# Splitting float64 weights in an attention and MoE kernel: sign by a parametric relu, low bits on GpSimd, and a new order of the opening

## The chip, the cores and the metric

The kernel runs on one core of a Trainium2 chip. The metric is the device time of one execution in microseconds (us); lower is better. TensorE is written PE, its weight loads PEld, VectorE DVE, ScalarE ACT, GpSimd POOL and the queue of the DMAs SP.

## The reference

Attention with a window of 128 keys and a distance bias for 8 batches, 8 heads, 576 positions and head width 64, then a gated layer: up-projection (512 to 1024), relu, a convolution over 3 tokens, a sigmoid gate, down-projection (1024 to 512). q, k and v are float32; the three weights are float64 words that have to become float32 on the chip.

```python
scores = scale * np.matmul(q, k.transpose(0, 1, 3, 2))
mask = (rel >= 0) & (rel < window)
scores = np.where(mask, scores + bias[None], -1000000000.0)
attn = softmax(scores)                      # max taken off, 1e-9 in the sum
x = (attn @ v), heads side by side          # 8 x 576 tokens, 512 wide
h = np.maximum(x @ w_in, 0.0)
for k in range(K):
    conv_out += conv_w[k][None, None, :] * hp[:, k:k + S, :]
gate = 1.0 / (1.0 + np.exp(-conv_out))
return (h * gate @ w_out).astype(np.float32)
```

## The kernel before

The 4608 tokens are 36 tiles t of 128 tokens; 18 chunks of 256 tokens go through the gated layer in 4 steps s each, a step being 256 of the 1024 hidden columns. Nothing is scheduled by a planner: three tables of names (`OPENING`, `PERIOD`, `TAIL`) are walked from left to right by `emit`, each name issues its instructions, and every engine runs its own in that order, one after another. `OPENING` covers tiles 0 to 10 and steps 0 to 10 and has all the weight work in it; `PERIOD` is repeated for two tiles and four steps at a time and has none; `TAIL` ends the program. Names that the text below uses:

- `LH`, `LD`, `LV`: DMAs of q and k, and of v, of one tile (tiles rqk and rv). From tile 9 on `LD` is 16 small DMAs. There are 3 buffers for rqk and 4 for rv.
- `QU`, `QV`: transposes of q and k on PE, and their copy on ACT; `S`: scores on PE; `MP`, `MB`: mask and bias with the row minimum, on DVE; `X`: exponentials on ACT; `N`: scaling of a row by its reciprocal sum, on DVE, ACT (4 instructions) or POOL; `T`, `RL`, `SEL`: transposes on PE, copy on ACT, select on POOL; `AV`: attention times v on PE. For tiles 9 and up `TQ` (DVE), `HQ` (ACT) and `LQ` (POOL or DVE) take the place of the transposes.
- `UH`: up-projection of half a step on PE; `HH`, `Z`, `CA`, `CB`, `TH`, `GT`, `GH`, `GL`: relu, convolution, gate and its split on ACT, DVE and POOL; `D`: down-projection on PE. Steps 0 to 3 multiply with the float32 weights wg, and later steps with a high part (wi, wo) and a low part (wl).
- `I`: idle matmuls on PE.

A float64 weight block b is 128 rows of 512 pairs of 32-bit words (blocks 0 to 3 and 5 to 8 are w_in, 4 is the small convolution weight, 9 to 16 are w_out), and each goes through: `F` its DMA (tile wst, 6 buffers), `CL` a clamp of the high words on POOL (L177), `RS` a scaling of them by 2 to the minus 112 into wg on ACT or POOL (L190, L188), `SG` a product with zero on POOL that leaves only the sign (L194), or `SH` a shift on DVE (L198) for two blocks, `V` two instructions on DVE: the low word's top 3 bits or'd with the sign (L209 or L213, into PSUM for blocks 0 to 6, else in place), and wg shifted by 3 and or'd with that (L216). `H` (ACT) and `W` (DVE or POOL, L235) make the high and low part.

One line of the queue's behaviour matters: `F`, `LD`, `LV` and the stores all stand in one queue on SP, where a DMA that waits for its buffer holds up all that stand behind it.

Of the kernel before, what the change touches and what calls it, by code (L numbers as in the profile page):

```python
# [944 lines left out]
```

## Time and profile before

| | before |
|---|---|
| median of 3 runs | 571.19 us (568.5 to 572.06) |
| the profiled execution | 568.98 us |
| its span, first to last instruction | 567.3 us |
| busy: PE, DVE, ACT, POOL | 558.1, 463.2, 430.6, 394.8 us |
| instructions | 16990 |

The profile is of one execution. Its time is 2.2 us below the median of the three runs and 1.7 us above its own span. An engine's busy time is the time in which it had an instruction in hand.

### The profile page before, as it was taken

What the parts mean: (1) busy time and instruction counts of PE and PEld (TensorE: products, weight loads), DVE (VectorE), ACT (ScalarE), POOL (GpSimd) and SP (SyncE); (2) the same over time, 40 slices, a digit from 0 to 9 for tenths busy, and PEclk for the clock granted to TensorE, in tenths of its full rate; (3) what the DMA queues carried; (4) which work ended last, traced back from release to release, by engine and by line L of the source; (5) the groups of instructions that cost most, each with busy time, mean ns of one, the idle gap of its engine ahead of it and who ended that gap; (6) DMA issues with size and microseconds to landing.
All of it is one profiled execution on the core that took longest, in us unless ns stands there. A gap on an engine that the chain in (4) does not pass through costs nothing.

```text
span 567.3 us, 16990 instructions
## 1 busy us (share of the span) xinstructions
PE 558.1 (98%) x6121; PEld 490.0 (86%) x6121; DVE 463.2 (82%) x1474; ACT 430.6 (76%) x1225; POOL 394.8 (70%) x453
## 2 busy tenths in 40 slices
...
GB/s 196 260 251 138 258 36 76 99 70 160 134 156 139 131 164 125 175 121 173 124 177 124 172 125 174 125 175 125 174 123 171 125 171 79 150 112 25 16 11 66
DMA packets 141225, 76.63 MB, mean 135 GB/s; under 512 B 116412, under 2 KB 131028, under 8 KB 141140
## 3 DMA queue, kind: packets, MB, share of 16 engines
...
## 4 chain that ended last, share of the span: by engine, by line
PE 91%; DVE 4%; DMA 2%; issue 1%; SPq 1%; ACT 0%; DVEq 0%
PE o L801 34%; PE p L698 34%; PE sc L387 8%; PE av L592 7%; PE o L791 2%; DMA rqk<-in_k_dram 2%; PE sc L432 2%; DVE sc L458 1%; PE av L632 1%; PE p L693 1%; SPq L320 1%; DVE wg L216 1%; PE pt L330 1%; DVE e L476 1%; DVE low L209 0%
## 5 line engine op out<-in xcount | busy, mean ns | idle before, releaser
L698 PE MATMUL p<-ring,wi 128*128 128x256 f32 x1088 | 195.4, 281 | 0.0
L731 DVE SCALAR_TENSOR_TENSOR zp<-hh,cw,zp 128x256 f32<-128x256 f32 (+7 forms) x384 | 160.5, 418 | 41.5 <-ACT zp L716 34.0
L698 PEld LDWEIGHTS p<-ring,wi 128*128 128x128 f32 x1088 | 168.7, 188 | 3.3 <-issue 0.2
L698 PE MATMUL p<-ring,wl 128*128 128x256 f32 x544 | 152.3, 280 | 0.0
L767 POOL TENSOR_TENSOR gl<-z,gh 128x512 fp32r<-128x512 f32 x67 | 86.8, 1296 | 79.9 <-ACT gh L758 79.1
L484 ACT ACTIVATE e<-e,st 128x128 f32<-128x128 f32 x288 | 112.7, 394 | 17.7 <-DVE st L476 17.4
L801 PE MATMUL o<-wo,gh 128*128 128x512 f32 x270 | 110.3, 409 | 0.0
L801 PE MATMUL o<-wo,gl 128*128 128x512 f32 x270 | 105.7, 392 | 0.0
L801 PE MATMUL o<-wl,gh 128*128 128x512 f32 x270 | 105.6, 391 | 0.0
L698 PEld LDWEIGHTS p<-ring,wl 128*128 128x128 f32 x544 | 102.7, 189 | 0.0
L716 ACT ACTIVATE zp<-hh,cw 128x256 f32<-128x256 f32 x144 | 68.9, 478 | 30.8 <-DVE z L746 20.2
L508 POOL TENSOR_TENSOR e<-e,st 128x512 f32<-128x512 f32 x60 | 62.4, 1041 | 15.1 <-DVE st L496 14.9
L368 POOL TENSOR_TENSOR qkT_low<-blk,qkT 128x1024 fp32r<-128x1024 f32 x25 | 59.9, 2397 | 16.8 <-ACT qkT L361 10.5
L476 DVE CUSTOM_DVE_ANT_0 e<-sc,bias 128x128 f32<-128x128 f32 x288 | 69.0, 285 | 1.1 <-DVE sc L458 0.2
L738 ACT ACTIVATE zp<-zp 128x512 f32<-128x512 f32 (+1 forms) x73 | 42.1, 577 | 33.3 <-DVE zp L731 33.1
L801 PEld LDWEIGHTS o<-wo,gh 128*128 128x128 f32 x270 | 50.6, 187 | 13.8 <-issue 0.2
L746 DVE SCALAR_TENSOR_TENSOR z<-zp,hh 128x512 f32<-128x512 f32 (+1 forms) x73 | 49.3, 676 | 14.1 <-ACT zp L738 12.3
L801 PEld LDWEIGHTS o<-wo,gl 128*128 128x128 f32 x270 | 50.6, 187 | 11.6
L710 ACT ACTIVATE hh<-p 128x512 f32<-128x512 f32 x67 | 40.0, 597 | 26.2 <-PE p L698 24.1
L801 PEld LDWEIGHTS o<-wl,gh 128*128 128x128 f32 x270 | 50.8, 188 | 9.5
L458 DVE COPY_PREDICATED sc<-m_prev,sc 128x256 f32<-128x256 uint8 x128 | 50.9, 420 | 8.9 <-PE sc L387 6.4
L484 ACT ACTIVATION_READ_ACCUMULATOR e<-e,st 128x1 f32 x288 | 54.3, 188 | 0.0
...
## 6 DMA issues: line engine op xcount, KB each, us to landing
...
rr<-scr SPq DMA_DIRECT2D x112, 128.0 KB
...
rqk<-in_q_dram SPq DMA_DIRECT2D x216, 32.0 KB
rqk<-in_k_dram SPq DMA_DIRECT2D x216, 32.0 KB
...
```

The lines of the kernel that those rows point to most:

```text
L368: eng.tensor_tensor(out=turned_of(qkT_low, t), in0=blks[t], in1=hi, op=ALU.subtract)
L387: nc.tensor.matmul(to, turned_of(tq, t)[rows, 0, g, b], of, start=n == 0, stop=n == len(passes) - 1)
L458: nc.vector.copy_predicated(out=s_cur, mask=mask.unsqueeze(1).to_broadcast(shp), data=data)
L476: nc.vector.tensor_tensor_reduce(out=e[:, j, :], in0=s_cur[:, g, :], in1=bias[:, head_of(t, u * HU + j), :], scale=-0.125, scalar=FAR, op0 ...
L484: nc.scalar.activation(out=e[:, j, :], in_=e[:, j, :], func=AF.Exp, bias=st[:, 0, j : j + 1], scale=-1.0, accum_out=st[:, 1, j : j + 1],)
L508: eng.tensor_tensor(out=e, in0=e, in1=st[:, 2, :].unsqueeze(2).to_broadcast([P, HU, P]), op=ALU.mult)
L698: nc.tensor.matmul(ps, a[:, part], ring[:, i, cc, cols], start=cc == 0 and n == 0, stop=cc == NCC - 1 and n == 2)
L716: nc.scalar.activation(out=zps[s][:, ff, :], in_=hhs[s][:, ff, 1 : 1 + CW], func=AF.Copy, scale=cw[:, 1, f : f + 1])
L731: nc.vector.scalar_tensor_tensor(out=z[:, ff, a:cut], in0=hh[:, ff, a + kk : cut + kk], scalar=cw[:, kk, f : f + 1], in1=z[:, ff, a:cut], ...
L746: nc.vector.scalar_tensor_tensor(out=zgs[s][:, ff], in0=zps[s][:, ff], scalar=1.0, in1=hhs[s][:, ff, 1 : 1 + CW], op0=ALU.add, op1=ALU.mult,)
L767: eng.tensor_tensor(out=gl, in0=zgs.pop(s), in1=as32(gh), op=ALU.subtract)
L801: nc.tensor.matmul(to, a[:, ff, ms], w[:, part], start=first and n == 0, stop=end and n == 2)
```

## The change

`RS` runs on ACT for all 17 blocks, as a parametric relu: a positive word is scaled by 2 to the minus 112 and a negative one by that times minus 2 to the 32, which puts one more bit in the exponent field, and that bit is the sign after the shift by 3. `SG` and `SH` are gone. A new `LW` on POOL multiplies the low word, as an unsigned integer, by 2 to the minus 29, bounds it by 7 and writes it back rounded to an integer. `V` is one instruction on DVE, and reads both its inputs from SBUF. No block's low bits go through PSUM any more.

The tables of who does what change too: six of the seven `N` that were on ACT leave it (one other comes), `N` on DVE grows from 5 to 10 in the opening, `W` on POOL goes from 10 blocks to 8, both `LQ` of tiles 9 and 10 are on POOL, and the low part of the gate of step 7 goes to DVE. `OPENING` is a new order of the same pieces; the number of `I` matmuls is the same.

```diff
-    LOW_PSUM = {0, 1, 2, 3, 4, 5, 6}
-    SIGNS = {0, 1, 2, 3, 5, 6, 7, 8, 9, 10, 11, 12, 13, 15, 16}
-    LOW_POOL = {2, 3, 7, 8, 9, 10, 11, 13, 14, 16}
-    RB_POOL = {0, 1, 3, 4, 5, 7, 9, 15}
-    N_ACT = {(1, 0), (2, 0), (3, 0), (4, 0), (4, 1), (5, 0), (5, 1)}
-    N_POOL = {(6, 0), (6, 1), (7, 0), (7, 1), (8, 0), (8, 1), (9, 0), (9, 1), (10, 0), (10, 1)}
-    GL_DVE = set()
+    LOW_POOL = {6, 8, 10, 11, 13, 14, 15, 16}
+    N_ACT = {(8, 0)}
+    N_POOL = {(1, 1), (4, 0), (5, 0), (5, 1), (7, 0), (7, 1), (8, 1), (9, 0), (9, 1), (10, 0), (10, 1)}
+    GL_DVE = {7}
-    LQ_DVE = {9, 10}
+    LQ_DVE = set()
...
-        if b in RB_POOL:
-            nc.gpsimd.tensor_scalar(out=g, in0=hf, scalar1=2.0**-112, scalar2=1.0, op0=ALU.mult, op1=ALU.mult)
-        else:
-            nc.scalar.activation(out=g, in_=hf, func=AF.Copy, scale=2.0**-112)
-
-    def w_sign(b):
-        hf = wst[b][..., 1].bitcast(F32)
-        nc.gpsimd.tensor_scalar(out=hf, in0=hf, scalar1=0.0, scalar2=0.0, op0=ALU.mult, op1=ALU.mult)
-
-    def w_shift(b):
+        nc.scalar.activation(out=g, in_=hf, func=AF.Prelu, scale=2.0**-112, alpha=-(2.0**32))
+
+    def w_low(b):
         lo = wst[b][..., 0]
-        nc.vector.tensor_scalar(out=lo, in0=lo, scalar1=29, scalar2=None, op0=ALU.logical_shift_right)
+        nc.gpsimd.tensor_scalar(out=lo, in0=lo, scalar1=2.0**-29, scalar2=7.0, op0=ALU.mult, op1=ALU.min)
 
     def w_bits(b):
         st, g = wst.pop(b), wgs[b]
...
         nc.vector.scalar_tensor_tensor(
-            out=g, in0=g, scalar=3, in1=low, op0=ALU.logical_shift_left, op1=ALU.bitwise_or
+            out=g, in0=g, scalar=3, in1=st[..., 0], op0=ALU.logical_shift_left, op1=ALU.bitwise_or
         )
...
-    LH0.0 QU0.0 LH0.1 LD1 F0 LD2 QU0.1 F4 QV0.0 LD3 CL0 CL4 S0.0 MP0.0.0 MB0.0.0 QV0.1 S0.1 F1 QU1.0 MP0.0.1 MB0.0.1
+    LH0.0 QU0.0 LH0.1 LD1 F0 LD2 QU0.1 F4 QV0.0 LD3 CL0 CL4 S0.0 MP0.0.0 MB0.0.0 QV0.1 S0.1 MP0.1.1 F1 QU1.0 MP0.0.1
```

What the new order means is best seen in the engines' own rows (in them a name's first number is the tile or block, and the last the buffer). The first place is SP's queue from the third w_in block to the block with number 2, before and then now:

```order
L170 DMA wst5_249<-in_moe_w_in_dram 128x1024
L320 DMA rqk4_263<-in_q_dram 64x8x64 x2
L320 DMA rqk4_263<-in_k_dram 64x8x64 x2
L320 DMA rv0_268<-in_v_dram 128x8x64
L170 DMA wst8_282<-in_moe_w_in_dram 128x1024
L170 DMA wst2_340<-in_moe_w_in_dram 128x1024
L320 DMA rqk5_353<-in_q_dram 128x8x64
L320 DMA rqk5_353<-in_k_dram 128x8x64
L320 DMA rv1_398<-in_v_dram 128x8x64
L320 DMA rv2_418<-in_v_dram 128x8x64
L170 DMA wst7_462<-in_moe_w_in_dram 128x1024
```

```order
L296 DMA rqk4_218<-in_q_dram 64x8x64 x2
L296 DMA rqk4_218<-in_k_dram 64x8x64 x2
L167 DMA wst5_223<-in_moe_w_in_dram 128x1024
L167 DMA wst8_227<-in_moe_w_in_dram 128x1024
L296 DMA rv0_230<-in_v_dram 128x8x64
L296 DMA rv1_298<-in_v_dram 128x8x64
L296 DMA rqk5_442<-in_q_dram 128x8x64
L296 DMA rqk5_442<-in_k_dram 128x8x64
L296 DMA rv2_445<-in_v_dram 128x8x64
L167 DMA wst2_477<-in_moe_w_in_dram 128x1024
L167 DMA wst7_514<-in_moe_w_in_dram 128x1024
```

Tile 4 of q and k moved ahead of weight block 5, weight block 8 ahead of the first v tile, and block 2 moved behind v of tiles 0 to 2 and q and k of tile 5.

The second place is POOL around the last step of block 2 before its merge, before (L194 is the sign) and then now (L188 is the low bits, L174 the clamp):

```order
L177 TENSOR_SCALAR wst2_340<-wst2_340 128x512
L525 AFFINE_SELECT rl2_1_543<-rl2_1_543 128x512
L528 AFFINE_SELECT rl2_1_543<-rl2_1_543 128x512
L194 TENSOR_SCALAR wst2_340<-wst2_340 128x512
L177 TENSOR_SCALAR wst7_462<-wst7_462 128x512
```

```order
L174 TENSOR_SCALAR wst5_223<-wst5_223 128x512
L174 TENSOR_SCALAR wst8_227<-wst8_227 128x512
L501 AFFINE_SELECT rl2_0_485<-rl2_0_485 128x512
L504 AFFINE_SELECT rl2_0_485<-rl2_0_485 128x512
L501 AFFINE_SELECT rl2_1_501<-rl2_1_501 128x512
L504 AFFINE_SELECT rl2_1_501<-rl2_1_501 128x512
L174 TENSOR_SCALAR wst2_477<-wst2_477 128x512
L174 TENSOR_SCALAR wst7_514<-wst7_514 128x512
L188 TENSOR_SCALAR wst2_477<-wst2_477 128x512
```

Block 2's last POOL step now stands behind the clamp of block 7, whose DMA comes after block 2's.

The third place is SP's queue later in the opening, before and then now:

```order
L320 DMA rqk8_1098<-in_q_dram 128x8x64
L320 DMA rqk8_1098<-in_k_dram 128x8x64
L285 DMA rqk9_1161<-in_q_dram 128x1x64 x8
L285 DMA rqk9_1161<-in_k_dram 128x1x64 x8
L285 DMA rqk10_1212<-in_q_dram 128x1x64 x8
L285 DMA rqk10_1212<-in_k_dram 128x1x64 x8
L320 DMA rv7_1431<-in_v_dram 128x8x64
```

```order
L296 DMA rqk8_1105<-in_q_dram 128x8x64
L296 DMA rqk8_1105<-in_k_dram 128x8x64
L296 DMA rv8_1180<-in_v_dram 128x8x64
L261 DMA rqk11_1256<-in_q_dram 128x1x64 x8
L261 DMA rqk11_1256<-in_k_dram 128x1x64 x8
L296 DMA rv7_1314<-in_v_dram 128x8x64
L261 DMA rqk9_1431<-in_q_dram 128x1x64 x8
L261 DMA rqk9_1431<-in_k_dram 128x1x64 x8
```

q and k of tile 9 moved behind v of tile 7, whose buffer is free when `AV` of tile 5 has read it on PE.

## Rows read from the trace of the kernel before

**Rows 1.** The page: busy time of each engine, share of the span, instructions.

```profile
PE 558.1 (98%) x6121; PEld 490.0 (86%) x6121; DVE 463.2 (82%) x1474; ACT 430.6 (76%) x1225; POOL 394.8 (70%) x453
```

**Rows 2.** Busy time by stage: the stretch, its length, the engines, clock, DMA share, GB/s.

```profile
0.00:20.00 20.00, 18.48 (x137) 15.45 (x138) 14.88 (x78) 14.35 (x52) 6.70 (x18) 1.00 0.92 226
20.00:39.00 19.00, 15.73 (x149) 12.02 (x148) 17.39 (x66) 17.59 (x66) 14.35 (x21) 0.91 0.97 246
39.00:62.00 23.00, 22.46 (x169) 18.03 (x168) 21.84 (x62) 21.47 (x67) 15.32 (x21) 1.00 0.71 162
62.00:540.00 478.00, 477.67 (x5534) 423.71 (x5533) 396.07 (x1243) 365.08 (x1019) 352.14 (x387) 1.00 0.50 131
540.00:567.30 27.30, 23.80 (x140) 20.84 (x138) 13.06 (x26) 12.11 (x26) 6.25 (x10) 1.00 0.11 40
```

**Rows 3.** The timeline of PE, 20 to 42 us: start, length, work, idle before.

```profile
23.74 0.41 PE L330 MATMUL pt<-ident_r,rqk 128*128 128x128 f32 x2 [1.06 <-DMA rqk<-in_k_dram]
...
25.08 2.08 PE L432 MATMUL sc<-qkT 64*128 64x256 f32 x8 [0.76 <-ACT qkT L336]
27.08 1.67 PE L632 MATMUL av<-rl,rv 128*64 128x128 f32 x16
...
33.16 3.71 PE L632 MATMUL av<-rl,rv 128*64 128x128 f32 x64
...
38.87 2.09 PE L693 MATMUL p<-x_first,wg 128*128 128x258 f32 x8
```

**Rows 4.** The timeline of DVE, 38 to 40 us: the merge of block 2.

```profile
39.08 0.69 DVE L216 SCALAR_TENSOR_TENSOR wg<-wg,low 128x512 uint32<-128x512 uint32 x1
```

**Rows 5.** The timeline of POOL, 31 to 38 us: clamps of blocks 2 and 7.

```profile
31.84 0.68 POOL L177 TENSOR_SCALAR wst<-wst 128x512 f32<-128x512 f32 x1
...
36.68 0.67 POOL L177 TENSOR_SCALAR wst<-wst 128x512 f32<-128x512 f32 x1
```

**Rows 6.** Groups by line and shape on DVE, first 150 us: busy us, mean ns.

```profile
L216 DVE SCALAR_TENSOR_TENSOR wg<-wg,wst 128x512 uint32<-128x512 uint32 x10 | 8.7, 868 | 0.4
L209 DVE SCALAR_TENSOR_TENSOR wst<-wst 128x512 uint32<-128x512 uint32 x9 | 6.2, 686 | 0.0
L348 DVE STREAM_TRANSPOSE blk<-rqk 128x1024 f32<-128x1024 f32 x4 | 5.0, 1238 | 0.2 <-DMA rqk<-in_k_dram 0.2
L209 DVE SCALAR_TENSOR_TENSOR low<-wst 128x512 uint32<-128x512 uint32 x6 | 4.9, 820 | 0.0
L216 DVE SCALAR_TENSOR_TENSOR wg<-wg,low 128x512 uint32<-128x512 uint32 x6 | 4.1, 688 | 0.3
...
L508 DVE TENSOR_TENSOR e<-e,st 128x512 f32<-128x512 f32 x5 | 3.5, 718 | 0.1
```

**Rows 7.** The same view of ACT.

```profile
L505 ACT ACTIVATE e<-e,st 128x128 f32<-128x128 f32 x28 | 8.9, 391 | 1.1 <-DVE st L496 1.1
...
L190 ACT ACTIVATE wg<-wst 128x512 f32<-128x512 f32 x9 | 6.1, 673 | 0.0
...
L361 ACT CAST qkT<-blk 128x1024 fp32r<-128x1024 f32 x4 | 4.2, 1038 | 0.0
```

**Rows 8.** The same view of POOL.

```profile
L194 POOL TENSOR_SCALAR wst<-wst 128x512 f32<-128x512 f32 x15 | 11.6, 780 | 8.3 <-ACT wg L190 8.0
...
L235 POOL TENSOR_TENSOR wl<-wg,wo 128x512 fp32r<-128x512 f32 x6 | 8.6, 1438 | 0.1
...
L368 POOL TENSOR_TENSOR qkT_low<-blk,qkT 128x1024 fp32r<-128x1024 f32 x2 | 4.8, 2404 | 1.6 <-DVE st L476 1.2 <-ACT qkT L361 0.3
```

**Rows 9.** The chain that ended last, 88 to 108 us: start, length, what.

```profile
88.90 3.64 PE av L632 x64
...
107.34 0.70 PE sc L387 x17
```

**Rows 10.** The timeline of SP's queue, 86 to 96 us.

```profile
86.07 4.49 SPq L285 DMA_DIRECT2D rqk<-in_q_dram  x8
90.60 4.56 SPq L285 DMA_DIRECT2D rqk<-in_k_dram  x8
```

More of the change, by code (lines that the diff above doesn't have):

```diff
@@ L844, in tile_alibi_window_attention_conv_glu @@
     }
-    WEIGHT = {"F": fetch_weight, "CL": w_clamp, "RS": w_rebias, "SG": w_sign, "SH": w_shift, "V": w_bits, "H": w_hi, "P": w_rest, "I": spin, "W": w_lo}
+    WEIGHT = {"F": fetch_weight, "CL": w_clamp, "RS": w_rebias, "LW": w_low, "V": w_bits, "H": w_hi, "P": w_rest, "I": spin, "W": w_lo}
     def emit(pieces, t=0, s=0):
@@ new lines, in tile_alibi_window_attention_conv_glu @@
+    MB0.0.1 X0.0.1 X0.0.0 MB0.1.1 RS0 MP0.1.0 MB0.1.0 F3 QU1.1 LD4 F5 LW0 CL1 F8 QV1.0 LV0 I2 I2 I2 QV1.1 I1 I1 S1.0
+    X0.1.1 X0.1.0 MP1.0.0 MB1.0.0 X1.0.0 S1.1 MP1.1.0 QU2.1 MP1.0.1 MB1.0.1 NR0 MB1.1.0 MP1.1.1 QU2.0 QV2.1 S2.1
+    QV2.0 S2.0 LV1 N0.1 N0.0 T0.0 RS4 LW4 X1.1.0 X1.0.1 MB1.1.1 X1.1.1 MP2.1.0 QU3.0 V4 CL3 MB2.1.0 T0.1 QU3.1 I1 RS1
+    NR1 QV3.0 N1.0 T1.0 RL0.0 MP2.0.1 N1.1 T1.1 MP2.0.0 LW1 X2.1.0 MP2.1.1 QV3.1 S3.1 RL1.0 RL0.1 SEL0.1 MB2.0.1
+    RL1.1 X2.0.1 MB2.0.0 X2.0.0 S3.0 SEL0.0 V0 SEL1.1 MP3.1.0 MB3.1.0 MB2.1.1 SEL1.0 QU4.0 MP3.0.0 X2.1.1 QV4.0 RS3
@@ new lines, in tile_alibi_window_attention_conv_glu @@
+    I1 MP3.1.1 MB3.1.1 MB3.0.0 MP3.0.1 MB3.0.1 NR2 QU4.1 QV4.1 X3.0.0 I2 LD5 LV2 X3.0.1 N2.0 P4 W4 S4.0 LW3 N2.1 AV0
+    XH0 MP4.0.1 MB4.0.1 F2 CL5 T2.0 RL2.0 V1 MP4.0.0 MB4.0.0 CL8 V3 T2.1 SEL2.0 RL2.1 S4.1 MP4.1.0 SEL2.1 F7 QU5.1
+    MP4.1.1 H0 MB4.1.0 X3.1.0 X3.1.1 NR3 F10 RS8 X4.0.1 CL2 AV1 CL7 RS5 N3.1 QV5.1 MB4.1.1 AV2 RS2 LW2 V2 CL10 XH1
+    XH2 XL2 LW5 N3.0 W0 X4.0.0 X4.1.1 H2 S5.1 MP5.1.1 T3.1 V5 RS7 LW7 UH1.0 HH1.0 MP5.1.0 H3 UH1.1 RL3.1 HH1.1 QU5.0
+    QV5.0 LW8 V8 UH0.0 MB5.1.1 X4.1.0 NR4 F6 LD6 T3.0 QU6.0 F12 RS10 H5 MB5.1.0 CL6 N4.0 RS6 LW6 LD7 HH0.0 S5.0 RL3.0
@@ new lines, in tile_alibi_window_attention_conv_glu @@
+    N4.1 H1 H8 QV6.0 MP5.0.0 UH0.1 HH0.1 V7 Z0.0 MP5.0.1 F11 KH6.0 T4.0 RL4.0 V6 QU6.1 QV6.1 LV4 CL12 CA0.0 CB0.0
+    Z0.1 LW10 V10 MB5.0.1 W5 CA0.1 UH3.0 UH2.0 HH3.0 X5.1.0 HH2.0 T4.1 RL4.1 MB5.0.0 CB0.1 TH0 SEL4.0 W3 S6.0 MP6.0.1
+    MB6.0.1 W1 GT0 SEL3.0 X5.1.1 SEL3.1 F16 LV3 SEL4.1 S6.1 MP6.1.0 MB6.1.0 X5.0.1 X5.0.0 LV6 NR5 Z1.0 MP6.1.1 KH6.1
+    KL6.1 CA1.0 MB6.1.1 X6.1.0 AV3 XH3 AV4 XH4 QU7.0 QV7.0 CB1.0 F9 KL6.0 CL11 H6 MP6.0.0 GL0 XL4 XL3 F14 CL9 UH2.1
+    QM7.0 Z1.1 CA1.1 RS9 XF4 RS12 CL16 KT6.1 QU7.1 MB6.0.0 RS16 KT6.0 UH3.1 CB1.1 F15 N5.1 H7 W2 TH1 GT1 LW12 LD10
@@ new lines, in tile_alibi_window_attention_conv_glu @@
+    LW9 V9 X6.1.1 T5.1 Z2.0 CA2.0 W7 HH2.1 CB2.0 CL15 RS11 UH4.0 UH4.1 QV7.1 QM7.1 HH3.1 LW11 UH5.0 N6.1 GL1 HH4 F13
+    LV5 RL5.1 SEL5.1 Z2.1 S7.0 S7.1 CL13 H9 CA2.1 CB2.1 W9 TH2 GT2 D0 V12 N5.0 T5.0 UH5.1 W6 W8 UH6.0 T6.1 X6.0.1
+    LW16 MP7.0.0 LD8 MB7.0.0 Z3.0 GL2 X6.0.0 CA3.0 MP7.1.1 CB3.0 Z3.1 RL5.0 RS13 SEL5.0 Q8 V11 RS15 MB7.1.1 CA3.1
+    CB3.1 TH3 MP7.1.0 MB7.1.0 HH5 H10 CL14 V16 UH6.1 W10 GT3 MP7.0.1 Z4.0 X7.1.1 RS14 MB7.0.1 CA4.0 CB4.0 Z4.1 LV8 D1
+    LW13 CA4.1 N6.0 T6.0 RL6.1 SEL6.1 QO8 LW14 CB4.1 V13 X7.0.1 TH4 GT4 H12 W12 RL6.0 SEL6.0 H13 W13 Z5.0 CA5.0
```

50 lines of the change are left out of this document (8 added, 42 removed).

## The prediction

> **What bounds the kernel now.** I read the page's busy times first, then the same times by stage, then the timelines of the engines where PE waits. The page shows PE busy for 98% of the span [rows 1]. So the change can only give back time in which PE has no work or works slowly, and the table by stage says where that is [rows 2]: from 62 to 540 us PE is busy 477.67 of 478 us, and all other engines have room there. What happens before 62 us moves the whole rest of the program by as much, and nothing behind it can be gained. The stages ahead leave little: PE lacks 1.5 us of the first 20, 3.3 of the next 19 and 0.5 of the next 23, together 5.3 us, the wait for the first data included. The last 3.5 us without PE are the end of the program, which the change doesn't touch. The timeline of PE names the waits after 20 us: a DMA of q and k, and twice ACT's copy, the first 0.76 us [rows 3]. After that the granted clock is at the lower of its two levels, 1.2 instead of 2.4 GHz, for a while (mean 0.91 from 20 to 39 us, 1.00 in the other stages [rows 2]): eight score matmuls take 2.08 us there, and the 16 matmuls of the first `AV` take 1.67, where 64 of the same take 3.71 later, so 0.93 for 16 [rows 3]. From 20 to 62 us DVE and ACT are busy over 91% [rows 2], that is, DVE and ACT set that stage's pace and PE follows.
>
> **What comes off the engines.** DVE loses one of two instructions per block: nine at 686 ns and six at 820 ns [rows 6], with the two blocks of another form some 12 us over the opening, and gets five `N` at 718 ns [rows 6], 3.6 us, and about as much in other moved subtractions as the two `LQ` that leave it: net some 8 to 10 us less. ACT loses six to seven `N` of four instructions at 391 ns each, which overlap a little, 1.3 us each and 8 us together, and gets eight `RS` at 673 ns, 5 us [rows 7]. POOL loses 15 `SG` at 780 ns and eight `RS`, 17 us, and gets 17 `LW` and two `LQ` at 2404 ns [rows 8], of which the second sum to 5 us. All of this lies beside PE's work: after 62 us it is worth nothing, and before 62 us it counts only in the 4 us that PE waits.
>
> The parametric relu is not in the trace. The nearest row is the scaling that it replaces, 673 ns, and I take that; above it the dearest ACT instruction of that width or twice it takes 1038 ns [rows 7], which for five blocks ahead of the first up-projection is under 2 us of ACT time; a cheaper one than the plain scaling has no reason. The low bits' product on unsigned integers isn't there either. Its nearest row is the sign's product, in place on the same words of the same tile, at 780 ns; the dearest single POOL instruction of that width, with two inputs, takes 1438 [rows 8]. I take 0.78 us and keep 1.44 as the upper end: the difference is 0.66 us on the way to one merge and 11 us spread over POOL's opening, where it was idle 5 us in 19 and 8 in 23 [rows 2].
>
> One observation speaks against the merge itself. With its second input in PSUM it takes 688 ns, with it in SBUF 868 [rows 6], on the same shapes. Seven blocks go from the first to the second, 7 x 0.18 = 1.3 us more on DVE, already within the net above. The Trainium skill, GPSIMD Engine Reference, Key points, says that GpSimd shares its SBUF interfaces with VectorE, and that they contend when a VectorE instruction has two SBUF inputs. The two means agree with it. If the rule bit on all 17 merges and on POOL's instructions as much, the sum would lose some 3 us on DVE of the 8 to 10, and the forecast time would stay, since DVE's work after 62 us is hidden.
>
> **First term: the start of the up-projection.** `UH` of step 1 is the first of eight pieces that need nothing but weights and x, and from its start at 38.87 us PE hardly waits again [rows 2, 3]. So the term is how much earlier it starts. Two things must be there.
>
> PE's own work ahead of it: from the first `AV` at 27.08 to 38.87 us are 11.8 us. In these are 1.4 us of waits (PE lacks 3.3 us from 20 to 39 us, 1.8 of them ahead of 27 [rows 2, 3]) and 0.74 us from the low clock (1.67 against 0.93). One of the transposes, 0.5 us, now stands ahead of `AV`. That leaves 9.2 us. `AV` needs v of tile 0, whose DMA now has block 8 ahead of it, 512 KB, or 2.1 us at 246 GB/s [rows 2]; before, it was there at 27.08 at the latest, without a wait. Tile 4 of q and k, that PE waited for, is as much earlier, but ahead of `AV` PE also needs free PSUM banks from DVE, as before. I take 27.4 us for `AV`, between 26.5 and 29.2. PE then arrives at `UH` at 36.6, between 35.7 and 38.4.
>
> Block 2, whose DMA moved back: the weight must be merged 0.93 us after `UH` starts, as the third of four row blocks. Before, its merge began at 39.08 and took 0.69 [rows 4]. Now its low bits are queued on POOL behind the clamp of block 7, which waits for block 7's DMA. As many bytes stand ahead of block 7 on SP's queue as before, 7.6 MB; at 226 and then 246 GB/s [rows 2] these are in at 32.6 us at the earliest, and at 36.68 at the latest, when its clamp ran before [rows 5]; block 2 itself was clamped by 31.84 then. I take the middle, 34.7. With a clamp of 0.67, the low bits 0.78, a merge of 0.87 and 0.3 for the handovers, the merge ends at 37.3, so `UH` may start at 36.4, between 34.3 and 39.0 (0.66 more at each end's dear side if the product takes 1.44).
>
> Both meet at about 36.6 us: **2.3 us** less than 38.87, between 3.2 less and 0.2 more. The half microsecond of waits from 39 to 62 us I leave as it is: with PE 2.3 us earlier, what DVE saves goes into keeping up.
>
> **Second term: tile 9.** The scores of tile 9 start at 107.34 us, and PE has run without a break since `AV` of tiles 5 and 6, which began at 88.90 and took 3.64 for two [rows 9]; from the end of `AV` of tile 5 at 90.7 to 107.3 are 16.6 us of PE's work, the same pieces in the new order. But v of tile 7 waits on SP's queue for just that `AV`, and the 16 DMAs of tile 9 now stand behind it. They take 4.49 + 4.56 us to issue [rows 10]. With 0.6 for v's own issue and 0.5 for the last landing, then `TQ` 1.24, `HQ` 1.04, `LQ` on POOL 2.40 [rows 6 to 8], and 0.9 in handovers, that is 15.7 us. The cover is 0.9 us, and ACT and POOL each run something else when their turn comes, up to 1.4 us. I take **0.5 us** of new waiting, between none and 3. What stands behind the wait on DVE (convolution and masks of the next tiles) has 15% of room after.
>
> **The sum** is 568.98 - 2.3 + 0.5 = 567.2 us against the profiled execution's own time. That execution lies 2.2 us under the median of the three runs; the mean of all four is 570.2, and I forecast on that footing: 570.2 - 1.8 = **568.5 us**, rounded.
>
> **The rivals.** (a) Nothing, within 0.6 us either way: the waits only change their names. For it: DVE and ACT still stand at over 90% ahead of 39 us, and moved `N` put 3.6 us back on DVE; block 2's upper bound is 39.0. It decides when block 7 lands after 36.5 us. Time 570. (b) Slower, by SP's queue: tile 9's scores come late because its DMAs wait for `AV` of tile 5. Against it stands 0.9 us of cover; it decides when the chain takes over 16.6 + 1.8 = 18.4 us, 2.7 more than summed, for example if the DMAs' issue is slowed by others in flight as much as the waits on ACT and POOL come together. At 20 us it costs 1.6 net, at 25 us 6.6: 572 to 577. (c) Slower, by an integer product that POOL does in software: at 1.44 us it is hidden, but POOL is idle only 12 us from 20 to 62 us and a quarter of the time after [rows 2], some 27 us up to 120, where the last weight is done: 1.6 for each of the 17, so it decides above 2.4 us for one. At 3.5 us it would be 17 x 1.1 = 19 us over, and half of it on PE's path makes 578. No row is near it. (d) The gain is larger than 1%: that is 5.7 us, out of the 5.3 that PE lacks ahead of 62 us and under 2 that the low clock took, the start included, so hardly more than the runs' scatter could show it. (e) The relu would need its own activation table: the built program has one table load, as before, so I give it nothing.
>
> The Trainium skill, ScalarE activation tables: per-element evaluation and per-set limits, says that with the same operands the instruction costs the same whichever table is read. By that the parametric relu takes 673 ns as the scaling does; no row here shows one.
>
> **How the numbers follow.** Runs of this kernel tell some 1% from no change, and my forecast is a third of that. Forecast (0.6 to 3.2 us less) 0.54; (a) 0.24; (b) 0.11, a third of it over 1%; (c) 0.06; (d) 0.05. So faster by over 1% 0.05, slower by over 1% 0.06 + 0.04 = 0.10, within 1% 0.85. The range is 565.5 (3.2 less than 570.2, and 1.5 of scatter as in the three runs) to 573 (2 more in (b), and some scatter).
>
> **What would show it.** In the profile after: `UH` of step 1 starts at 36 to 37 us; PE is idle under 2.5 us from 20 to 39; the low bits take about 0.8 us, the relu 0.67; the scores of tile 9 start 16.6 to 17.1 us after `AV` of tile 5 ends, with `LQ` as what they waited for; after 62 us PE lacks under 1 us elsewhere. The prediction is wrong if PE waits for weights between 39 and 107 us, if the low bits take over 2.5 us, or if the clock drops again after 30 us.

## Result, and the profile after

The changed kernel takes **573.49 us** (median of 10 runs, 572.43 to 575.12) against 569.80 for the kernel before (10 runs, 568.50 to 572.06): ratio 1.0064, 95% interval 1.0045 to 1.0084. So it is within 1%, as forecast, but on the slow side: 3.7 us more where 1.8 less was expected, and half a microsecond beyond the upper end of the range. The profiled execution took 573.1 us with a span of 571.1.

The page's busy times after, to hold against [rows 1]:

```profile
PE 558.4 (98%) x6121; PEld 491.8 (86%) x6121; DVE 452.8 (79%) x1461; ACT 428.8 (75%) x1209; POOL 417.6 (73%) x447
```

DVE lost 10.4 us, as planned, PE's work is the same, and POOL, which was to stay about even, gained 22.8. The stages show where that mattered (stretch, length, engines, clock, DMA share, GB/s, as in [rows 2]):

```profile
0.00:20.00 20.00, 16.66 (x120) 14.46 (x121) 12.94 (x71) 13.24 (x46) 6.87 (x16) 1.00 0.93 218
20.00:39.00 19.00, 17.87 (x169) 13.95 (x168) 16.59 (x69) 18.21 (x66) 18.25 (x19) 1.00 1.00 252
39.00:62.00 23.00, 19.81 (x128) 16.35 (x130) 18.31 (x49) 16.16 (x48) 21.95 (x18) 0.93 0.80 207
62.00:540.00 478.00, 476.49 (x5540) 422.40 (x5537) 390.43 (x1247) 366.93 (x1022) 363.38 (x387) 1.00 0.51 129
```

From 20 to 62 us POOL is busy 40.2 of 42 us, where it had idle time to give in [rows 2]. PE gained 2.1 us from 20 to 39, and then lost 2.65 from 39 to 62, 1.2 behind 62, and 1.8 in the first 20. The groups of the new operations in the first 130 us (busy us, mean ns of one, idle time ahead and who ended it) name the cause, for POOL, ACT and DVE in turn:

```profile
L188 POOL TENSOR_SCALAR wst<-wst 128x512 uint32<-128x512 uint32 x16 | 35.3, 2206 | 1.2
```
```profile
L184 ACT ACTIVATE wg<-wst 128x512 f32<-128x512 f32 x16 | 10.6, 674 | 3.4 <-POOL wst L174 3.2
```
```profile
L192 DVE SCALAR_TENSOR_TENSOR wg<-wg,wst 128x512 uint32<-128x512 uint32 x16 | 12.5, 779 | 8.0 <-POOL wst L188 8.0
```

The relu (L184) takes the 674 ns that the scaling took. The low bits (`LW`, L188) take 2.21 us each, where 0.78 was expected; 16 of the 17 blocks have the full width, and their 16 products make the 22.8 us that POOL gained (16 x 1.43). DVE stands 8.0 us in front of its merges (L192) for them. How such a wait reaches PE is seen in three timelines (start, length, work, idle time ahead). POOL first:

```profile
36.15 2.31 POOL L188 TENSOR_SCALAR wst<-wst 128x512 uint32<-128x512 uint32 x1
...
39.80 7.13 POOL L188 TENSOR_SCALAR wst<-wst 128x512 uint32<-128x512 uint32 x3
```

Then DVE, the merges of blocks 2 and 8:

```profile
38.50 0.69 DVE L192 SCALAR_TENSOR_TENSOR wg<-wg,wst 128x512 uint32<-128x512 uint32 x1 [1.47 <-POOL wst L188]
...
46.96 0.69 DVE L192 SCALAR_TENSOR_TENSOR wg<-wg,wst 128x512 uint32<-128x512 uint32 x1 [3.10 <-POOL wst L188]
```

And PE:

```profile
37.57 1.04 PE L669 MATMUL p<-x_first,wg 128*128 128x258 f32 x4
39.24 2.88 PE L669 MATMUL p<-x_first,wg 128*128 128x258 f32 x12 [0.64 <-DVE wg L192]
...
42.40 1.91 PE L669 MATMUL p<-x_first,wg 128*128 128x258 f32 x8
...
48.13 1.62 PE L408 MATMUL sc<-qkT 64*128 64x256 f32 x8 [2.95 <-DVE st L452]
49.68 3.59 PE L669 MATMUL p<-x_first,wg 128*128 128x258 f32 x8
```

`LW5`, `LW7` and `LW8` stand on POOL's queue in a row and end at 46.93. The merge `V8` waits for the third, and DVE works in order: `MB5.1.1`, which stands behind `V8`, is what frees the PSUM bank for `S5.0`. So PE, at 48.13, waits 2.95 us for a softmax step (L452) that has nothing to do with the weights. Afterwards the granted clock is at the lower of its two levels for a while, 0.50 of full speed in the stretch from 50 to 53 us (columns as in [rows 2]):

```profile
50.00:53.00 3.00, 3.00 (x8) 2.23 (x7) 2.93 (x6) 1.13 (x3) 2.86 (x3) 0.50 1.22 285
```

Eight matmuls take 3.59 us there, where eight of the same took 1.91 at 42.40. A last wait comes at 94.82 us (`AV6`): POOL's mask step of tile 6 (L504) stands behind the product of a late block.

```profile
91.33 2.02 POOL L188 TENSOR_SCALAR wst<-wst 128x512 uint32<-128x512 uint32 x1
...
94.12 0.64 POOL L504 TENSOR_SCALAR_AFFINE_SELECT rl<-rl 128x512 f32<-128x512 f32 x1
```
```profile
94.82 1.97 PE L608 MATMUL av<-rl,rv 128*64 128x128 f32 x32 [1.30 <-POOL rl L504]
```

### The profile page after: what moved, and what is told of

It reads as the page before. It is cut to its first block, busy times and chain, and to the rows that moved or that the text cites. A ratio compares the mean times of both kernels' runs of the same rounds, so it can differ in the third digit from the quotient of the medians.

```text
span 571.1 us, 16956 instructions
## 1 busy us (share of the span) xinstructions
PE 558.4 (98%) x6121; PEld 491.8 (86%) x6121; DVE 452.8 (79%) x1461; ACT 428.8 (75%) x1209; POOL 417.6 (73%) x447
## 4 chain that ended last, share of the span: by engine, by line
PE 83%; POOL 12%; SPq 2%; DMA 1%; issue 1%; DVE 0%; POOLq 0%
PE o L777 34%; PE p L674 32%; PE sc L363 8%; PE av L568 7%; POOL wst L188 5%; POOL wst L174 2%; POOL rl L504 2%; POOL rl L501 2%; DMA wst<-in_moe_w_in_dram 1%; PE o L767 1%; SPq L296 1%; SPq L167 1%; POOL wl L211 1%; POOL e L484 1%; PE av L608 1%
## 5 line engine op out<-in xcount | busy, mean ns | idle before, releaser
L743 POOL TENSOR_TENSOR gl<-z,gh 128x512 fp32r<-128x512 f32 x66 | 85.3, 1292 | 78.7 <-ACT gh L734 77.6
L344 POOL TENSOR_TENSOR qkT_low<-blk,qkT 128x1024 fp32r<-128x1024 f32 x27 | 64.8, 2398 | 19.1 <-ACT qkT L337 13.3
L484 POOL TENSOR_TENSOR e<-e,st 128x512 f32<-128x512 f32 x61 | 64.5, 1058 | 11.4 <-DVE st L472 10.0
L452 DVE CUSTOM_DVE_ANT_0 e<-sc,bias 128x128 f32<-128x128 f32 x288 | 69.1, 286 | 1.0
```

Source lines behind the costliest of these rows:

```text
L344: eng.tensor_tensor(out=turned_of(qkT_low, t), in0=blks[t], in1=hi, op=ALU.subtract)
L452: nc.vector.tensor_tensor_reduce(out=e[:, j, :], in0=s_cur[:, g, :], in1=bias[:, head_of(t, u * HU + j), :], scale=-0.125, scalar=FAR, op0 ...
L484: eng.tensor_tensor(out=e, in0=e, in1=st[:, 2, :].unsqueeze(2).to_broadcast([P, HU, P]), op=ALU.mult)
L743: eng.tensor_tensor(out=gl, in0=zgs.pop(s), in1=as32(gh), op=ALU.subtract)
```

## The experiments

### What makes the low bits dear: first round

**e1: float words in place of unsigned ones.**

```diff
-        lo = wst[b][..., 0]
-        nc.gpsimd.tensor_scalar(out=lo, in0=lo, scalar1=2.0**-29, scalar2=7.0, op0=ALU.mult, op1=ALU.min)
+        lo, hi = (wst[b][..., i].bitcast(F32) for i in range(2))
+        nc.gpsimd.tensor_scalar(out=lo, in0=hi, scalar1=0.0, scalar2=7.0, op0=ALU.mult, op1=ALU.min)
```

> The changed kernel with its low-bits step on GpSimd working on float32 in and out (the high words times 0.0, bounded by 7), as many elements and the same place of output; the low 3 bits of the weights are left out. Theory 1 (the integer product at 2.21 us is the whole loss; the new order is sound): the step takes 0.65 to 0.8 us, GpSimd is idle again from 20 to 62 us, the time is 566 to 569 us, 1 to 4 less than before. Theory 2 (the order itself costs: later scores early on, moved DMAs, more scaling on VectorE): the step gets cheap, but the time stays at 572 to 574. Theory 3 (tile 9's DMAs behind v of tile 7): TensorE waits over 1 us ahead of the scores of tile 9 as soon as the rest is faster.

Measured: 574.09 us, ratio 1.0079 (1.0048 to 1.0110). The group of the low bits on float words:

```profile
L188 POOL TENSOR_SCALAR wst<-wst 128x512 f32<-128x512 f32 x16 | 35.5, 2219 | 1.2
```

The price stays with float words, which none of the three theories had expected, and the time with it. "A product on integers is slow" is refuted: whatever makes this instruction dear, it isn't the unsigned words.

**e2: the low bits as a shift on DVE**, POOL freed of them.

```diff
-        nc.gpsimd.tensor_scalar(out=lo, in0=lo, scalar1=2.0**-29, scalar2=7.0, op0=ALU.mult, op1=ALU.min)
+        nc.vector.tensor_scalar(out=lo, in0=lo, scalar1=29, scalar2=None, op0=ALU.logical_shift_right)
```

> The changed kernel with the low bits made by a logical shift on VectorE (one instruction of about 0.75 us ahead of each merge) instead of GpSimd; nothing is left out. Theory 1: GpSimd loses 36 us, VectorE gets 12, the waits on the low bits go, 567 to 570 us. Theory 2: 572 to 575, since the order is kept and VectorE has more to do.

Measured: 572.60 us, ratio 1.0050 (1.0031 to 1.0069). The stage from 39 to 62 us (columns as in [rows 2]):

```profile
39.00:62.00 23.00, 21.45 (x166) 17.71 (x165) 22.58 (x68) 19.27 (x58) 13.59 (x18) 1.00 0.85 219
```

Now POOL is idle 9.4 of 23 us, and DVE has 0.4 us left. The loss moves to the other engine; it doesn't go away, as theory 2 said. The run can't tell whether the order is at fault or only the second engine without room.

**e3: the price by types**, one for each block, so its time is no measure.

```diff
...
+        elif b == 1:
+            nc.gpsimd.tensor_scalar(out=lo.bitcast(F32), in0=lo, scalar1=0.0, scalar2=7.0, op0=ALU.mult, op1=ALU.min)
...
+        elif b == 7:
+            nc.gpsimd.tensor_scalar(out=lo, in0=lo, scalar1=2.0**-29, scalar2=None, op0=ALU.mult)
...
```

> The changed kernel with another form of the low-bits step for each block, to price it; the weights' low bits are wrong in some blocks. Same 128x512 elements on GpSimd: uint32 to uint32 with product and bound (block 0 and 9 to 16), uint32 to float32 (1), float32 to uint32 (2), uint16 to uint32 (3), uint8 to uint32 (5), int32 to int32 (6), uint32 to uint32 with the product alone (7), float32 to float32 (8). If the integer read is what is slow, 1 is near 2.2 us and 2 near 0.7; if the rounding write is, the other way round; if the second operation is, 7 is cheap; if narrow integers are cheaper, 3 and 5 lie under 1.5.

Measured, POOL's groups (L205 is float to float; L197 reads 16-bit words; L203 is the multiplication with no second operation; L175 is the clamp, limit and limit, in the same run):

```profile
L175 POOL TENSOR_SCALAR wst<-wst 128x512 f32<-128x512 f32 x16 | 12.6, 797 | 10.1 <-DMA wst<-in_moe_w_in_dram 9.7
L197 POOL TENSOR_SCALAR wst<-wst 128x512 uint32<-128x512 uint16 x1 | 2.5, 2521 | 0.1
...
L203 POOL TENSOR_SCALAR wst<-wst 128x512 uint32<-128x512 uint32 x1 | 2.1, 2120 | 0.1
...
L205 POOL TENSOR_SCALAR wst<-wst 128x512 f32<-128x512 f32 x1 | 2.0, 2012 | 0.1
```

Every type costs 2.0 to 2.5 us, while the clamp on the same tiles takes 0.80. Leaving the second operation out doesn't help either (2.12), so the limit isn't dear by itself. What differs from the clamp is the pair of operations. The sign's product of before, at 780 ns [rows 8], was a pair too: multiply, multiply.

**e4: the new order and its tables with the old arithmetic**: the sign's product in `LW`'s place and two DVE instructions a block again. It isn't the kernel before in another order and nothing else: the scaling is on ACT for all blocks, and the low bits stay in SBUF.

```diff
-        nc.scalar.activation(out=g, in_=hf, func=AF.Prelu, scale=2.0**-112, alpha=-(2.0**32))
+        nc.scalar.activation(out=g, in_=hf, func=AF.Copy, scale=2.0**-112)
...
-        lo = wst[b][..., 0]
-        nc.gpsimd.tensor_scalar(out=lo, in0=lo, scalar1=2.0**-29, scalar2=7.0, op0=ALU.mult, op1=ALU.min)
+        hf = wst[b][..., 1].bitcast(F32)
+        nc.gpsimd.tensor_scalar(out=hf, in0=hf, scalar1=0.0, scalar2=0.0, op0=ALU.mult, op1=ALU.mult)
...
+        lo, hi = st[..., 0], st[..., 1]
+        nc.vector.scalar_tensor_tensor(
+            out=lo, in0=lo, scalar=29, in1=hi, op0=ALU.logical_shift_right, op1=ALU.bitwise_or
+        )
```

> The new order and the new tables with the old arithmetic: plain scaling on ScalarE, the sign by a float product on GpSimd where the low-bits step stands, two instructions per block on VectorE; nothing is left out. Theory 1: near the run with the shift, 567 to 571 us, since GpSimd is cheap again and VectorE does 12 us more. Theory 2: 572 to 575.

Measured: 577.65 us, ratio 1.0145 (1.0109 to 1.0182). The stage from 39 to 62 us:

```profile
39.00:62.00 23.00, 18.82 (x110) 15.02 (x112) 22.52 (x56) 14.98 (x41) 13.32 (x16) 1.00 0.87 232
```

DVE is full and PE lacks 4.2 us; the loss is larger than either theory had it. So the new order with its tables, which also give DVE five more `N`, is worse than the old one as long as DVE keeps both instructions of a block. Whether it is good with what it was written for needed a cheap low-bits instruction.

### The pair of operations: second round

**e7: two factors instead of a factor and a limit.** The second factor brings the largest value, 8 after rounding, to 7.499, so that it rounds to 7; every smaller value rounds at most one step of the low bits differently.

```diff
-        nc.gpsimd.tensor_scalar(out=lo, in0=lo, scalar1=2.0**-29, scalar2=7.0, op0=ALU.mult, op1=ALU.min)
+        nc.gpsimd.tensor_scalar(out=lo, in0=lo, scalar1=2.0**-29, scalar2=0.9374, op0=ALU.mult, op1=ALU.mult)
```

> The changed kernel with one thing else: the low bits as a product of two factors (2^-29, then 0.9374, so that the largest rounds to 7) instead of a factor and an upper limit; words and types as before. Theory 1 (the pair of operations sets POOL's price; multiply, multiply is the pair of the sign's product that took 0.78 us, multiply and limit took 2.0 to 2.5 us whatever the type): about 0.7 us each, DVE's merges wait under 2 us for POOL instead of 8, up-projection of step 1 at 36.6 us, time 566 to 569. Theory 2 (integer words or unsigned rounding are slow on POOL as well): about 2.1 us and 573 to 575. Theory 3 (the new order itself costs, as with the old arithmetic): cheap product, yet 571 to 575.

Measured: **566.96 us** (6 runs, 566.35 to 567.39), ratio 0.9945 (0.9925 to 0.9966). The group, the stages, and the places on POOL, DVE and PE that cost the changed kernel its time:

```profile
L188 POOL TENSOR_SCALAR wst<-wst 128x512 uint32<-128x512 uint32 x16 | 12.9, 808 | 1.2
```
```profile
0.00:20.00 20.00, 16.96 (x122) 14.81 (x123) 13.10 (x71) 12.73 (x45) 5.27 (x15) 1.00 0.96 219
20.00:39.00 19.00, 17.87 (x169) 14.12 (x168) 18.07 (x71) 18.79 (x69) 17.06 (x22) 1.00 0.97 255
39.00:62.00 23.00, 22.95 (x176) 19.28 (x175) 22.07 (x67) 21.03 (x62) 17.65 (x23) 1.00 0.79 217
```
```profile
36.68 3.25 POOL L188 TENSOR_SCALAR wst<-wst 128x512 uint32<-128x512 uint32 x3
```
```profile
42.71 0.68 DVE L192 SCALAR_TENSOR_TENSOR wg<-wg,wst 128x512 uint32<-128x512 uint32 x1
```
```profile
11.97 2.00 PE L408 MATMUL sc<-qkT 64*128 64x256 f32 x16 [1.39 <-ACT qkT L312]
...
26.39 1.31 PE L408 MATMUL sc<-qkT 64*128 64x256 f32 x8
27.63 1.09 PE L608 MATMUL av<-rl,rv 128*64 128x128 f32 x16
...
45.84 2.01 PE L669 MATMUL p<-x_first,wg 128*128 128x258 f32 x8
```

The same three products take 3.25 us in a row instead of 7.13, `V8` begins at 42.71 without a wait, PE has 22.95 of 23 us, and the clock is 1.00 throughout. One operation and its constant in one instruction make 6.5 us of span (571.1 to 564.6). By the stages, PE stands still 4.6 us less ahead of 540 us (4.6 against 9.2 us) and is busy 1.9 us less (556.5 against 558.4), which is the 6.5. The largest parts are in the rows: 2.95 at `S5.0`, 1.58 of low clock in the eight matmuls behind it (3.59 against 2.01), 1.30 at `AV6`, 0.64 less 0.31 around `UH` of step 1, and 0.30 in the first 20 us. This is theory 1, except that `UH` of step 1 begins at 38.11 and not at 36.6 us. This version beats both kernels, the kernel before by half a percent.

**e8: the sign's old product in that place.**

```diff
-        lo = wst[b][..., 0]
-        nc.gpsimd.tensor_scalar(out=lo, in0=lo, scalar1=2.0**-29, scalar2=7.0, op0=ALU.mult, op1=ALU.min)
+        lo, hi = (wst[b][..., i].bitcast(F32) for i in range(2))
+        nc.gpsimd.tensor_scalar(out=lo, in0=hi, scalar1=0.0, scalar2=0.0, op0=ALU.mult, op1=ALU.mult)
```

> The changed kernel with the sign's old product (float words, two factors of zero) in the place of the low bits' product, written to the low word; it leaves out the low three bits of the weights. Theory 1 and 2 both: 0.65 to 0.8 us each; if the price of the low bits is the whole loss, 566 to 569 us and the first scores of step 5 without the 2.9 us wait. Theory 3 (the order costs by itself): 571 to 575 with the price gone.

Measured: 567.32 us, ratio 0.9949 (0.9931 to 0.9967), 819 ns each: the same as e7 on other types. The type makes no difference on the cheap side either.

**e9: prices of nine kinds**, each on one or more types, one for each block.

```diff
...
+        if b == 0:
+            nc.gpsimd.tensor_scalar(out=lo, in0=lo, scalar1=2.0**-29, scalar2=0.9374, op0=ALU.mult, op1=ALU.mult)
...
+        elif b == 2:
+            nc.gpsimd.tensor_scalar(out=lo.bitcast(F32), in0=hi, scalar1=0.0, scalar2=0.0, op0=ALU.min, op1=ALU.max)
...
+        elif b == 8:
+            nc.gpsimd.tensor_scalar(out=lo.bitcast(F32), in0=hi, scalar1=0.0, scalar2=0.0, op0=ALU.max, op1=ALU.min)
...
```

> Prices only, one pair of operations for each block of the changed kernel (the low bits are left out in most blocks): multiply, multiply on unsigned, on float, and between them; limit, limit on float (both orders) and unsigned; multiply, limit; limit, multiply; multiply, add; multiply alone. Theory 1 (pair): multiply, multiply and limit, limit take 0.65 to 0.85 us for every type, the mixed pairs and the single multiply 2.0 to 2.4. Theory 2 (unsigned words): every instruction that reads or writes unsigned words takes over 2 us, every float one under 0.9, which the float multiply, limit at 2.2 already speaks against.

Measured, POOL's groups. L189, L207: multiply, multiply (unsigned, float to unsigned; on float words it took 676 ns). L195, L193: lower limit after upper (min, max; unsigned, float). L201: multiply, add. L203: max, min. L215: multiply, min. L197: multiply, max. L205: multiply alone. Left out here are max, multiply (2017 ns) and min, multiply (2477 ns).

```profile
L215 POOL TENSOR_SCALAR wst<-wst 128x512 uint32<-128x512 uint32 x3 | 6.4, 2129 | 0.2
L197 POOL TENSOR_SCALAR wst<-wst 128x512 f32<-128x512 f32 x1 | 2.5, 2484 | 0.0
...
L203 POOL TENSOR_SCALAR wst<-wst 128x512 f32<-128x512 f32 x1 | 2.0, 2049 | 0.0
...
L205 POOL TENSOR_SCALAR wst<-wst 128x512 f32<-128x512 f32 x1 | 1.6, 1615 | 0.0
L207 POOL TENSOR_SCALAR wst<-wst 128x512 uint32<-128x512 f32 x1 | 1.0, 994 | 0.1
L201 POOL TENSOR_SCALAR wst<-wst 128x512 f32<-128x512 f32 x1 | 0.7, 714 | 0.0
...
L193 POOL TENSOR_SCALAR wst<-wst 128x512 f32<-128x512 f32 x1 | 0.7, 688 | 0.0
...
L189 POOL TENSOR_SCALAR wst<-wst 128x512 uint32<-128x512 uint32 x1 | 0.7, 662 | 0.1
L195 POOL TENSOR_SCALAR wst<-wst 128x512 uint32<-128x512 uint32 x1 | 0.7, 661 | 0.1
```

Two groups with nothing between 1.0 and 1.6 us: multiply, multiply; min, max; and multiply, add take 0.66 to 0.99 us, everything else 1.6 to 2.5. The order of the two counts: min, max takes 688 ns, max, min 2049. And the single multiplication is dearer than two in one instruction. The expectation had multiply, add on the dear side and limit, limit on the cheap one in both orders; both were wrong. Each price here is one instruction, or three.

**e10: the new arithmetic with the cheap product, in the old order and with the old tables.** In the kernel before, `RS` becomes the relu on ACT for every block, `SG` and `SH` become the product of e7, and `V` the single merge.

```diff
-        if b in RB_POOL:
-            nc.gpsimd.tensor_scalar(out=g, in0=hf, scalar1=2.0**-112, scalar2=1.0, op0=ALU.mult, op1=ALU.mult)
-        else:
-            nc.scalar.activation(out=g, in_=hf, func=AF.Copy, scale=2.0**-112)
+        nc.scalar.activation(out=g, in_=hf, func=AF.Prelu, scale=2.0**-112, alpha=-(2.0**32))
...
```

> The new arithmetic with the low bits as two factors, in the order and with the tables of the kernel before (relu on ScalarE for all blocks, the low bits where the sign's product or the shift stood). Theory 1: low bits at 0.7 us, DVE some 12 us less busy, 566 to 569 us. Theory 2: over 2 us each and 572 to 577. Theory 3 (order): this one is faster than the changed kernel's order with the same product by 2 us or more.

Measured: 574.62 us, ratio 1.0085 (1.0061 to 1.0109). The products are cheap (0.73 us in the mean), and it is slower than both the kernel before and e7, which none of the three theories had. So the same arithmetic is 1.4% apart in the two orders, each with its tables. With e4 that makes four corners against the kernel before: old order and old arithmetic 1, new order with old arithmetic 1.0145, old order with new arithmetic 1.0085, both new 0.9945. Neither half gained by itself, as far as e4 and e10 part them. What the old order does wrong with the relu, ACT's timeline and then PE's:

```profile
10.55 0.66 ACT L187 ACTIVATE wg<-wst 128x512 f32<-128x512 f32 x1 [1.97 <-POOL wst L177]
```
```profile
11.73 1.88 PE L413 MATMUL sc<-qkT 64*128 64x256 f32 x8 [2.62 <-ACT qkT L317]
```

Before, the scaling of block 0 stood on POOL (`RB_POOL`). Its relu now stands on ACT, waits 1.97 us for the clamp of that block, and holds up the copy of q and k for which PE waits 2.62 us. PE's waits for that copy (L317) come to 7.2 us in five places. At three of them, 4.8 us, a relu stands on ACT just ahead of the copy or a little before it, behind a wait for its clamp; at the other two, 2.4 us, the exponentials stand there, and for those copies PE waited before too (0.76 and 0.97 us). The 4.8 us is most of the 5.1 by which the span grew.

### Which products cost, and why the old order lost: third round

**e11: the dear pair in blocks 6 and 9 to 16 alone** (the edit against e7).

```diff
+        if b in (6, 9, 10, 11, 12, 13, 14, 15, 16):
+            nc.gpsimd.tensor_scalar(out=lo, in0=lo, scalar1=2.0**-29, scalar2=7.0, op0=ALU.mult, op1=ALU.min)
+        else:
             nc.gpsimd.tensor_scalar(out=lo, in0=lo, scalar1=2.0**-29, scalar2=0.9374, op0=ALU.mult, op1=ALU.mult)
```

> The changed kernel with the cheap product of two factors, except in blocks 6 and 9 to 16, which have the slow multiply, limit (some 2.1 us against 0.8, 12 us more on GpSimd, nearly all behind 45 us). Theory 1 (the loss is made ahead of 62 us, where GpSimd had no room, and behind that GpSimd has slack): within 0.7 us of the run with cheap products everywhere, 566.5 to 567.7, and no wait of PE for the relocated weights' transposes at AV of tile 6. Rival 1b (the wait of 1.3 us at AV of tile 6 comes from the late slow products by themselves): 568 to 569.

Measured: 569.20 us, ratio 1.0005 (0.9993 to 1.0017), where e7 has 0.9945; the spans differ by 2.1 us. PE, at `AV6`:

```profile
90.40 1.97 PE L611 MATMUL av<-rl,rv 128*64 128x128 f32 x32 [1.29 <-POOL rl L507]
```

The rival was right, and the time is 0.2 us above the 569 that it gave: the wait comes without any dear product among the early blocks. With two shorter ones of the same kind at 54.7 and 56.4 us (0.26 and 0.53) that is the 2.1 us. The late dear products alone eat the whole gain of e7, even where PE seemed safe.

**e12: the complement**, blocks 0 to 5, 7 and 8 dear (the edit against e11).

```diff
-        if b in (6, 9, 10, 11, 12, 13, 14, 15, 16):
+        if b in (0, 1, 2, 3, 4, 5, 7, 8):
```

> The complement: blocks 0 to 5, 7 and 8 slow, the others cheap. Theory 1: these eight make the loss: VectorE's merge of block 8 waits 2.5 to 3.5 us behind three products in a row, the scores of step 5 wait 2 to 3 us, the clock falls for the matmuls behind them (8 in 3.6 us instead of 1.9), together 4.5 to 6 us: 571.5 to 573. Rival 1b (the loss is spread over all 17): half of it, 569.5 to 570.5.

Measured: 573.07 us, ratio 1.0073 (1.0049 to 1.0097). DVE at `V8`, and PE at `S5.0`:

```profile
46.63 0.69 DVE L195 SCALAR_TENSOR_TENSOR wg<-wg,wst 128x512 uint32<-128x512 uint32 x1 [3.08 <-POOL wst L189]
```
```profile
47.80 1.68 PE L411 MATMUL sc<-qkT 64*128 64x256 f32 x8 [2.93 <-DVE st L455]
```

Theory 1 was right: these eight alone cost what all 17 cost, within the runs' intervals, by the waits seen in the changed kernel. Whether the two parts add the runs don't tell: by the ratios they are 1.3% and 0.6% over e7 and 1.2% together, by the spans of the profiled executions 4.9 and 2.1 of 6.5 us.

**e13: the old order of e10 with the normalisations off ACT**, as the changed kernel's tables have them: all seven `N` that ACT had leave it, and one other comes.

```diff
-    N_ACT = {(1, 0), (2, 0), (3, 0), (4, 0), (4, 1), (5, 0), (5, 1)}
+    N_ACT = {(8, 0)}
...
```

> The run with the new arithmetic, cheap products and the old order (574.6 us, where PE waited 7.2 us for ScalarE's copies), with one thing else: the normalisations that ScalarE had for tiles 1 to 5 go to VectorE and GpSimd, as the changed kernel's tables have them. Theory 4 (the old order lost because eight relus came to ScalarE and nothing left it): PE's waits for ScalarE fall under 3 us and the time to 566 to 570. Rival (the order of the pieces itself, whatever the engines' loads): 572 to 575 still.

Measured: 579.49 us, ratio 1.0202 (1.0185 to 1.0219). Theory 4, ACT's load, falls; the rival's sign is right, but its 572 to 575 are too low. PE's waits:

```profile
PE sc L413 <- ACT qkT L317: 7.1, 5, 2.4
PE pa L495 <- POOL e L489: 3.0, 1, 3.0
```

The five waits for the copies stay as they were, with less work on ACT, and the moved normalisations bring one on POOL. ACT still stands 5.9 us, in five places, in front of relus whose block isn't clamped yet. So what is left as the likely cause is where the relus stand in ACT's queue, the reading of e10; that was read from the traces and not tried by itself.

**e14: e7 with the copies of tile 1 ahead of the exponentials of tile 0 on ACT.** The idle matmuls around them move too, and four of them go (24 in the place of 28).

```diff
...
-    MB0.0.1 X0.0.1 X0.0.0 MB0.1.1 RS0 MP0.1.0 MB0.1.0 F3 QU1.1 LD4 F5 LW0 CL1 F8 QV1.0 LV0 I2 I2 I2 QV1.1 I1 I1 S1.0
+    MB0.0.1 QV1.0 QV1.1 X0.0.1 X0.0.0 MB0.1.1 RS0 MP0.1.0 MB0.1.0 F3 LD4 F5 LW0 CL1 F8 LV0 I2 S1.0
...
```

> The cheap product with one more edit: ScalarE copies q and k of tile 1 before it takes the exponentials of tile 0, so that the scores of tile 1 need not wait 1.4 us at 11.97 us (ScalarE idles from 7.0 to 9.2 us there). If that wait bounds the opening: the scores of tile 1 start at 9 to 10.5 us and the time falls by 0.7 to 1.5 us to 565.5 to 566.3. If the transfers of the next tiles or the exponentials behind bound it: 566.5 to 567.5, the wait reappears at tile 2.

Measured: 566.40 us, ratio 0.9957 (0.9942 to 0.9972): no different from e7, and between the two forecasts. PE:

```profile
14.67 2.00 PE L408 MATMUL sc<-qkT 64*128 64x256 f32 x16 [1.01 <-ACT qkT L312]
...
21.19 0.66 PE L490 MATMUL pa<-ident_r,e 128*128 128x128 f32 x4 [1.02 <-POOL e L484]
```

The wait of 1.4 us at 12 us is gone, and two of 1.0 us come at tile 2 and behind it. The opening is held by more than that copy.

## Why the prediction was wrong, by its own steps

**The step that failed** is the price of the low bits: "I take 0.78 us and keep 1.44 as the upper end". It measured 2.21. The row that it took, the sign's product on the same words, was the right row for width, tile and engine, and e7 shows 0.81 on unsigned words once the pair is the sign's pair. What the prediction didn't look at was the one thing that differed from that row besides the type: the second operation. It worried about integers (rival c), which cost nothing (e1, e8). The extra 1.43 us times 16 is 23 us on POOL, and e7 shows that this alone is the way from 0.9945 to 1.0064.

**The threshold of rival (c)** failed as well. The products were to decide "above 2.4 us for one", from 27 us of POOL's idle time up to 120 us, shared among 17. At 2.21 they already cost 6.5. The idle time was summed over a stretch in which it can't be moved: three products stand in a row ahead of `V8`, and that row had to be done by 42.7 us. The mechanism of (c), POOL without room, was right, with a cause that wasn't integers; its price, 8 us at 3.5 us a product, no run tests.

**The relu** took 674 ns, as the scaling did [rows 7]. The Trainium skill (ScalarE activation tables: per-element evaluation and per-set limits, What a function is on this engine) says that with the same operands the instruction costs the same whichever table is read; the 674 and 673 ns agree with that. The relu brought no second table load: the trace of the changed kernel has one, as before.

**DVE's net** of 8 to 10 us less: 10.4 measured, a little more. The merges took 0.78 us, and 0.82 in e7, between the two rows that the prediction had for them [rows 6]; how much of that comes from POOL's use of SBUF at the same time, no run parts.

**The first term**, `UH` of step 1 at 36.6 us: it began at 37.57, waited 0.64 us inside for block 2, and even with the cheap product it begins at 38.11 in e7. The first `AV` came as forecast, at 27.38 us (27.63 in e7), but from it to `UH` are 10.2 us (10.5 in e7), waits included, where the prediction summed 9.2. So the term was mis-sized at its place: 0.8 us in e7 instead of 2.3. The gain came nevertheless with the cheap product, and larger than the 1.8 us of the sum: 2.7 of span in e7. That the total comes out near the forecast there is luck, since it stands elsewhere: PE has 2.1 us more than before from 20 to 39 and 0.5 more from 39 to 62 [rows 2], the clock is no longer low (some 1.4 us, from the 2.08 and 1.67 of [rows 3] against 1.31 and 1.09 in e7), and PE has 1.5 less in the first 20 us. That loss at the start, in a stretch that the prediction passed over, is for the most part a wait of 1.39 us of the first scores of tile 1 for ACT's copy, at 11.97 us in e7.

**The second term**, tile 9: forecast 0.5, measured none. SP's queue, POOL and PE in the changed kernel:

```profile
93.56 0.37 SPq L296 DMA_DIRECT2D rv<-in_v_dram  x1
...
98.54 4.85 SPq L261 DMA_DIRECT2D rqk<-in_k_dram  x8
```
```profile
109.26 2.40 POOL L344 TENSOR_TENSOR qkT_low<-blk,qkT 128x1024 fp32r<-128x1024 f32 x1
```
```profile
111.53 0.47 PE L363 MATMUL sc<-qkT 32*128 32x128 f32 x4
```

The v of tile 7 is issued as `AV5` ends (93.52), the 16 DMAs go out behind it, and the low part (`LQ9`) ends at 111.66 as the scores begin, with no wait recorded on PE. From `AV5`'s end that is 18.1 us where 15.7 were summed; the cover was longer too, 18.0 us, by the 1.30 that PE waited at `AV6`. In e7 the scores begin some 16.5 us after `AV5`, and the chain ends with them: it just fits there too. Its term that was furthest off is the last landing, 2.0 us in e7 (issue ended at 98.19, `TQ9` begins at 100.23) where 0.5 was taken. Rival (b) didn't come, by a narrow margin: it was to decide above 18.4 us.

**After 62 us** the prediction took everything as hidden. For DVE and ACT that held. For POOL it didn't: PE loses 1.3 us at `AV6`, and e11 shows that late products alone do it. PE's 477.67 of 478 us in [rows 2] says that nothing was late with the old prices; it doesn't say how much later a step could be.

**The signs named** for being right held for the relu and for PE's idle time from 20 to 39 us (1.13 us). They didn't hold for `UH` of step 1 (37.57 us), for the low bits, for the scores of tile 9 (18.0 us after `AV` of tile 5, with no wait for `LQ`), and for PE behind 62 us, which lacks 1.5 us to 540. Of those for being wrong two came: PE waited for a weight up to 39.24 us, and the clock fell again after 30 us. The bound of 2.5 us for one product wasn't passed in the mean: it stood too high, as rival (c)'s threshold did.
